# Strassen's seven products for the first MLP matrix of a transformer block, and one written list of the MLP's instructions

## Chip, cores and metric

The kernel runs on one core of a Trainium2 chip. A core has a matrix engine (TensorE, PE in the profile), a vector engine (VectorE, DVE), a scalar engine (ScalarE, ACT), GpSimd (POOL), and queues that start DMA transfers, here mostly SyncE's (SP). Each engine works through its own list of instructions in order and waits for the others by semaphores. The metric is the device time of one execution in microseconds (us).

## What is computed

One transformer block on S = 2048 tokens of width D = 640: a modulated LayerNorm, attention over a sliding window of 256 tokens with 32 heads, a residual, a second modulated LayerNorm, and an MLP with its own LayerNorm, width FF = 1536 and a GELU. All is in float32. Cut to what matters here:

```python
h = _layernorm(x) * (1 + ca) + sa
x = x + ga * _A_ref(h, A_wqkv, A_wo)          # attention, output projection
h = _layernorm(x) * (1 + cb) + sb
y = _layernorm(h)
g = gelu(y @ w1 + b1)                          # 640 -> 1536
x = x + gb * (g @ w2 + b2)                     # 1536 -> 640
```

## The kernel before

**Products in three parts.** Float32 operands are split into a high part (rounded to the matmul's type) and a low part (the rest). Each product is then three matmuls: high x high, high x low, low x high. So every operand that is made on the way costs a copy (the high part, on ScalarE or VectorE) and a subtraction (the low part, on VectorE or GpSimd).

**Tiles.** 128 tokens are a block (16 of them, `bg`), 512 tokens a chunk (4, `ch`). D is 5 tiles of 128 (KT), FF is 12 (FT). A matmul of the MLP streams 512 columns, the tokens of a chunk.

**Stages.** Attention runs first, in slots counted by `t`. Near its end the blocks of tokens go through `mid_steps(bg)` (L826): load the attention output and `x` ("load"), scale (`om`), split (`oh`, `ol`), output projection (`w00` to `w14`, ten steps of three matmuls of 320 columns), add to `x` (`add0`, `add1`), statistics (`sa0`, `sa1`), normalize (`n1`, ScalarE), modulate (`m0`, `m1`), transposes of `x` and their store (`x0`, `x1`), statistics again (`sb0`, `sb1`), normalize (`n2`), transposes of `y` and their split (`y0`, `y0l`, `y1`, `y1l`). Blocks 0 to 3 do this in the attention's last slots, block 4 partly; the others run between the matmuls of the MLP, at times from the table `MID_AT`, in units of a block: `mids` holds the steps, `fill()` hands one out after each group of three matmuls.

**MLP.** A loop over the four chunks and over the 12 tiles `f` of FF. For each: w2's tile is loaded and split, 15 matmuls make `h` (5 tiles of depth, 3 parts) in the one PSUM bank "h", ScalarE makes the GELU, VectorE splits `g`, and meanwhile `second` adds the previous `f` into the five banks `out` (15 matmuls). w1 is loaded and split once, in chunk 0, and all of its 12 tiles stay in SBUF. `close` scales the result, adds the residual and stores it. The modulation vector `gb` is made during chunk 0 (`gate`).

**What sets the order.** The attention's order comes from tables (`EXTRA`, `EARLY`, `WARM` and others). In the MLP it is the loop's order, with `mids` put in by time; on VectorE, ScalarE and GpSimd it is the order in which the program issues the instructions.

Of the kernel before, what the change touches and what calls it, by code (L numbers as in the profile page):

```python
# [35 lines left out]
MODV = 133  # L36
# [10 lines left out]
MV = [8, 9, 12, 17, 19, 21, 22, 26, 28, 29, 30]  # L47
# [16 lines left out]
SUMS_LAST = [14, 15, 18, 25, 26, 27, 29, 35, 42, 43, 50, 59, 63, 64, 74, 76, 79, 83, 86, 88, 91, 92, 95, 101, 105, 106, 110, 111, 113, 116, 117, 118, 120, 121, 122, 123, 126, 129, 131, 132, 133, 135, 136, 139]  # L64
# [5 lines left out]
WOS = [89.75, 94.0, 99.5, 109.0, 111.75, 114.25, 117.5]  # L70
W1S = [117.75, 121.75, 133.75]
# [7 lines left out]
LO0 = 4.5  # L79
PER = 4.8132  # L80
LATE = 0.8265
TAIL_AT = {'rd': -1.338, 'ri': -0.963, 'load': -0.933, 'om': -0.141, 'oh': 0.058, 'ol': 0.133, 'w00': 0.287, 'w01': 0.36, 'w02': 0.382, 'w03': 0.493, 'w04': 0.511, 'add0': 0.569, 'sa0': 0.741, 'w10': 0.711, 'w11': 0.716, 'w12': 0.726, 'w13': 0.855, 'w14': 0.865, 'add1': 0.885, 'sa1': 1.178, 'n1': 1.2, 'm0': 1.327, 'x0': 1.382, 'x1': 1.544, 'm1': 1.344, 'sb0': 1.562, 'sb1': 1.598, 'n2': 1.709, 'y0': 1.844, 'y0l': 2.007, 'y1': 2.026, 'y1l': 2.118}
MID_AT = {'rd': -1.42, 'ri': -0.884, 'load': -0.74, 'om': -0.25, 'oh': 0.081, 'ol': 0.084, 'w00': 0.336, 'w01': 0.341, 'w02': 0.367, 'w03': 0.455, 'w04': 0.495, 'add0': 0.567, 'w10': 0.643, 'sa0': 0.626, 'w11': 0.736, 'w12': 0.773, 'w13': 0.837, 'w14': 0.924, 'add1': 0.968, 'sa1': 1.042, 'n1': 1.181, 'm0': 1.223, 'm1': 1.236, 'x0': 1.314, 'sb0': 1.338, 'x1': 1.465, 'sb1': 1.467, 'n2': 1.504, 'y0': 1.802, 'y0l': 1.925, 'y1': 2.011, 'y1l': 2.093}
# [3 lines left out]
        "w12 w13,w13 w14,w14 add1,add0 sa0,sa0 sa1,add1 sa1,sa1 n1,n1 m0,m0 m1,m0 sb0,m1 sb1,sb0 sb1,sb1 n2,n2 y0,y0 y0l,"  # L87
        "y0 y1,y1 y1l,x0 x1,add1 x0,y0l y1"
# [33 lines left out]
def block_kernel(ctx: ExitStack, tc: tile.TileContext, x, wqkv, wo, w1, b1, w2, b2, c, crow, wmod, wcol, sel, outT):  # L122
# [410 lines left out]

# [25 lines left out]

# [251 lines left out]
    def r_steps(ch):  # L811

        ts, box = slice(ch * CHUNK, (ch + 1) * CHUNK), {}

        def load():
            pool, tag = (att, "rd") if ch < 2 else (base, "acc")
            box["rd"] = pool.tile([P, P if ch < 2 else D], F32, tag=tag, name=f"rd{ch}")[:, 0:P]
            nc.sync.dma_start(box["rd"], o_scr[:, DH, ts])

        def invert():  # L820
            nc.vector.reciprocal(box["rd"], box["rd"])
            nc.sync.dma_start(r_scr[:, ts], box["rd"])

        return load, invert

    def mid_steps(bg):  # L826
# [20 lines left out]
        def o_low():  # L847
            nc.gpsimd.tensor_tensor(bx["oT"][1], bx["o"], f32(bx["oT"][0]), ALU.subtract)
# [21 lines left out]
        def stats(src, nm, h):  # L870
            mid = box2["mid"]
            if h == 0:
                bx["st"] = mid.tile([P, 2, 6], F32, tag="st", bufs=2, name=f"st{nm}{bg}")
            st = bx["st"]
            nc.vector.bn_stats(st[:, h], src[:, 320 * h : 320 * h + 320])
            if h == 0:
                return
            mv = mid.tile([P, 2], F32, tag="mv", bufs=3, name=f"mv{nm}{bg}")
            rs = mid.tile([P, 1], F32, tag="rs", bufs=3, name=f"rs{nm}{bg}")
            nc.vector.bn_aggr(mv, st)  # L880
            rstd_of(rs, mv[:, 1:2])
            nr = mid.tile([P, 1], F32, tag="nr", bufs=3, name=f"nr{nm}{bg}")
            nc.gpsimd.tensor_tensor(nr, mv[:, 0:1], rs, ALU.mult)
            nc.gpsimd.tensor_scalar(nr, nr, -1.0, None, ALU.mult)
            bx[nm] = nr, rs

        def apply_(dst, src, nm):
            nr, rs = bx[nm]
            nc.scalar.activation(dst, src, AF.Identity, bias=nr, scale=rs)

        def norm1():
            bx["y"] = box2["mid"].tile([P, D], F32, tag="yb", name=f"y{bg}")
            apply_(bx["y"], bx["x"], "a")

        def mod(h):
            y, cs = bx["y"][:, 320 * h : 320 * h + 320], slice(320 * h, 320 * h + 320)
            eng = nc.vector if now[0] >= MODV and bg < len(TAIL0) or 2 * bg + h in MV else nc.gpsimd
            eng.tensor_tensor(y, y, box2["cb"][:, cs], ALU.mult)
            eng.tensor_tensor(y, y, box2["sb"][:, cs], ALU.add)

        def xtrans(k0, k1):
            def go():
                if k0 == 0:
                    bx["xT"] = box2["mid"].tile([P, KT, P], F32, tag="xT", name=f"xT{bg}")
                nc.scalar.copy(bx["xT"][:, k0:k1], turned(bx["x"], f"xt{bg}", k0, k1))
                if k1 == KT:
                    nc.sync.dma_start(x1_scr[:, :, rows].rearrange("k p t -> p k t"), bx["xT"])

            return go

        def ytrans(k0, k1):
            cs = slice(bl * P, (bl + 1) * P)

            def go():
                if ch < 2 and ch not in yT:
                    yT[ch] = [base.tile([P, KT, CHUNK], F32R, tag=f"h{i}{1 - ch}", name=f"y{i}{ch}") for i in ("hi", "lo")]
                bx["py", k0] = turned(bx["y"], f"yt{bg}", k0, k1)
                nc.scalar.copy(yT[ch % 2][0][:, k0:k1, cs], bx["py", k0])
# [574 lines left out]
```

## Time and profile before

| | |
|---|---|
| median of 3 runs | 978.35 us (977.57 to 978.8) |
| span of the profiled execution, first to last instruction | 975.4 us |
| PE busy | 945.9 us, 97% of the span |
| VectorE, ScalarE, GpSimd busy | 589.0, 445.1, 487.8 us |
| first matmul of the MLP's first product | at 576.9 us |
| matmuls of 512 columns in the MLP | 720 of the first product, 720 of the second |
| PE's mean granted clock | 0.998 |

The profile comes from one execution, and its span leaves out what lies around the first and the last instruction; its own full time is not given. A busy PE is not a PE at its peak, since matmuls overlap and their ends are modelled: how often one starts is what counts. The names in a row are those of the program's tiles, out<-in; all instructions have the line of one helper (L116), so they are told apart by tile.

### The profile page before, as it was taken

The page shows a single profiled execution, that of the slowest core. Times are in us where ns is not written, and L with a number is a line of the kernel's source. Part 1 is how long each engine was busy: PE and PEld are TensorE (multiplying, and loading weights), DVE is VectorE, ACT ScalarE, POOL GpSimd, SP SyncE. Part 2 cuts the span into 40 slices and gives each one's busy share as a digit, 9 for nine tenths or more (in the row PEclk, how much of TensorE's full clock was granted, in tenths as well). Part 3 has the DMA queues.
Part 4 walks back from the last instruction along what each step waited for, and adds up shares of the span by engine and source line. Part 5 has one row for each costly group of instructions (what it writes and reads, how often), then busy time and mean ns, then how long its engine had stood idle before and what let it go on. Part 6 is the DMA issues. An engine that isn't in the chain of part 4 may idle for free.

```text
span 975.4 us, 20091 instructions
## 1 busy us (share of the span) xinstructions
PE 945.9 (97%) x7781; PEld 751.9 (77%) x7781; DVE 589.0 (60%) x991; ACT 445.1 (46%) x781; POOL 487.8 (50%) x674
## 2 busy tenths in 40 slices
PE   8899999999999999999889999999999999999998
PEld 8777777777777777777677677888888888888886
DVE  6564977888776786767788556563544344342112
ACT  3723555666654545555545654434333243333222
POOL 3423555677864364463646844654454454332121
PEclk9999999999999999999999999999999999999999
DMA  8366778666778359854862245444413342124113
GB/s 307 97 210 197 244 228 274 188 187 170 220 226 251 114 175 283 240 157 120 226 161 76 81 142 156 127 130 138 138 57 103 115 145 85 54 58 144 54 43 119
DMA packets 98974, 152.17 MB, mean 156 GB/s; under 512 B 8864, under 2 KB 42112, under 8 KB 98880
## 3 DMA queue, kind: packets, MB, share of 16 engines
q1 hardware_dynamic: 89664, 142.50, 48.4%
q10 hardware_dynamic: 9216, 8.39, 2.7%
q8 instruction: 62, 1.02, 0.4%
q14 instruction: 32, 0.26, 0.1%
HBM read 98.51 MB, written 51.58 MB: 154 GB/s over the span
## 4 chain that ended last, share of the span: by engine, by line
PE 81%; DVE 7%; ACT 5%; DMA 2%; issue 2%; POOL 1%; SPq 1%; ACTq 0%; DVEq 0%; POOLq 0%
PE pp L116 17%; PE out L116 16%; PE h L116 16%; PE e L116 8%; PE o L116 7%; PE wo L116 6%; PE s L116 4%; ACT pt L116 3%; DVE e L116 2%; PE ppo L116 1%; SPq L116 1%; PE yt L116 1%; DVE nm L116 1%; DMA wc<-in_wcol 1%; PE xt L116 1%
## 5 line engine op out<-in xcount | busy, mean ns | idle before, releaser
L116 POOL TENSOR_SCALAR_AFFINE_SELECT pt<-pt 128x512 f32<-128x512 f32 x192 | 129.1, 672 | 128.8 <-ACT pt L116 122.0
L116 ACT ACTIVATE pt<-e 128x1024 f32<-128x1024 f32 (+1 forms) x120 | 133.7, 1114 | 64.5 <-DVE e L116 62.0
L116 DVE TENSOR_REDUCE nm<-s 128x1 f32<-128x256 f32 (+4 forms) x206 | 157.6, 796 | 4.4
L116 POOL TENSOR_TENSOR w2lo<-w2r,w2hi 128x640 fp32r<-128x640 f32 x48 | 78.5, 1635 | 163.0 <-ACT w2hi L116 163.0
L116 PE MATMUL e<-qbuf,kbuf 62*128 62x128 f32 (+2 forms) x773 | 111.8, 328 | 10.6 <-ACT pt L116 9.5
L116 DVE CAST ghi<-g 128x512 fp32r<-128x512 f32 x48 | 27.4, 571 | 155.0 <-ACT g L116 155.0
L116 PEld LDWEIGHTS e<-qbuf,kbuf 62*128 62x128 f32 x773 | 80.8, 185 | 49.8 <-ACT pt L116 25.9
L116 PE MATMUL pp<-hhi,w_hi 128*128 128x512 f32 x265 | 113.6, 429 | 0.2 <-ACT pf L116 0.2
L116 PE MATMUL s<-kbuf,qbuf 60*128 60x384 f32 (+2 forms) x728 | 105.9, 302 | 4.3 <-DVE nm L116 1.9
L116 PE MATMUL pp<-hlo,w_hi 128*128 128x512 f32 x265 | 108.3, 409 | 0.6 <-POOL hlo L116 0.6
L116 DVE COPY_PREDICATED e<-mask_t,e 128x512 f32<-128x512 uint32 x96 | 66.6, 694 | 70.0 <-PE e L116 65.8
L116 PE MATMUL pp<-hhi,w_lo 128*128 128x512 f32 x265 | 106.2, 401 | 0.0
L116 PE MATMUL o<-pt,vbuf 128*32 128x128 f32 x2688 | 99.6, 277 | 0.6 <-ACT xT L116 0.6
L116 PEld LDWEIGHTS s<-kbuf,qbuf 60*128 60x128 f32 x728 | 89.1, 186 | 14.2 <-DVE nm L116 5.9
L116 PE MATMUL out<-ghi,w2hi 128*128 128x512 f32 x240 | 95.3, 397 | 0.9 <-ACT g L116 0.9
L116 PE MATMUL out<-glo,w2hi 128*128 128x512 f32 x240 | 93.9, 391 | 0.0
L116 PE MATMUL out<-ghi,w2lo 128*128 128x512 f32 x240 | 93.8, 391 | 0.0
L116 POOL TENSOR_TENSOR w_lo<-wraw,w_hi 128x128 fp32r<-128x128 f32 x171 | 76.1, 476 | 31.4 <-ACT w_hi L116 31.4
L116 PE MATMUL h<-yhi,w1hi 128*128 128x512 f32 x220 | 87.6, 398 | 0.0
L116 PE MATMUL h<-ylo,w1hi 128*128 128x512 f32 x220 | 86.1, 392 | 0.0
L116 PE MATMUL h<-yhi,w1lo 128*128 128x512 f32 x220 | 86.0, 391 | 0.0
L116 DVE COPY_PREDICATED s<-mask_t,s 128x512 f32<-128x512 uint32 x112 | 77.1, 688 | 13.8 <-PE s L116 13.5
(179 smaller groups left out, 1838.3 us busy)
## 6 DMA issues: line engine op xcount, KB each, us to landing
w2r<-in_w SPq DMA_DIRECT2D x48, 320.0 KB
qbuf<-q_scr SPq DMA_DIRECT2D x60, 240.0 KB
wraw<-in_wqkv SPq DMA_DIRECT2D x36, 320.0 KB
kbuf<-k_scr SPq DMA_DIRECT2D x44, 240.0 KB
q_scr<-stage SPq DMA_DIRECT2D x20, 512.0 KB
k_scr<-stage SPq DMA_DIRECT2D x20, 512.0 KB
o_scr<-oT ACTq DMA_DIRECT2D x64, 128.0 KB
wm<-in_wmod SPq DMA_DIRECT2D x20, 320.0 KB
```

The source lines that it names most:

```text
L116: return self.tc.keep_in_program_order(op(*args, **kw))
```

## The change

The first product of the MLP is made for two chunks, A and B, at once. With w1 cut into two halves of FF (6 tiles each, `HF`) and the depth cut into tiles 0 and 1 on one side and 2, 3, 4 on the other, it is a 2 x 2 block product, and Strassen's scheme (in the form of Winograd) makes it of seven products, P1 to P7, instead of eight:

- P1 and P2 use w1 and chunk A as they are. P1 is copied to SBUF (`p1`), P2 is added to it (`a2`), which gives the first six tiles of A.
- P3 to P7 use sums and differences of w1's blocks (`w1_sums` on VectorE or GpSimd, five instructions; split by `ws_high`, `ws_low`) and of the chunks' blocks (`combine`: `raw`, `t1`, `t2`, `t3`, `t4` and the split of t1 and t2; `ra`, `th`, `tl` for chunk A's side). Their results are put together by `a6`, `a7`, `b5`, `a5`, `a4`, `a3` (VectorE, one operand in PSUM), and the GELU follows (`e5`, `e4`, `e3`).

For each pair of chunks there are three parts: the P1/P2 part, with chunk A's second product; the middle part with P6, P5, P7, P4, P3 for each of six `i` (54 matmuls each, 15 of them of the second product); and a last part with the second product of chunk B alone. P1, P2, P4, P6 and P7 use the bank "h", P5 and P3 the bank "t".

w1 no longer stays in SBUF: it is loaded and split again for each pair. `mid_steps` is cut into finer pieces; `n1` goes, and `m0` and `m1` become one VectorE instruction each over 640 columns, with the normalization in them; the scaling `om` and the low parts `ol` go to VectorE for some blocks.

The instructions of the MLP are one list, `PLAN`: a word is one step, a number is that many groups of three matmuls. Some entries of the attention's tables (`SUMS_LAST`, `WARM`, `WOS`, `W1S`, `TAIL_AT`, `NEXT`) shift as well.

```diff
-WARM = {(115, 0): 2, (121, 0): 2, (127, 2): 1, (130, 1): 4, (135, 0): 5, (136, 0): 10}
+WARM = {(115, 0): 1, (121, 0): 3, (127, 2): 1, (130, 1): 2, (135, 0): 4, (136, 0): 10, (114, 3): 6, (120, 3): 1, (135, 2): 1}
-NEXT = 134.05
-CROSS = 1.07
+NEXT = [133.869, 138.565]
+CROSS = [1.165, -0.035]
+PLAN = """
+w1d2 w2d1 gl3 gl4 gl0 gl2 load.6b gl1 1 w1h01 1 w2h0 m0.4 x0.4a p100 w2l0 w1l01 w1h02 w2h1 m1.4 1 w1d3 oh.5 w2d2
...
+"""
+COMB = {"raw": "p", "t1": "p", "t1h": "d", "t1l": "d", "t3": "p", "t2": "p", "t2h": "d", "t2l": "d", "t4": "p"}
+SPAN = [0, 0, 0, 0, 0, 2, 1, 1, 0, 0, 0, 0, 0, 2, 1, 1]
+OME = 'pppdpppppddddddp'
+OLE = 'pppppdpdpddddddd'
...
         def mod(h):
-            y, cs = bx["y"][:, 320 * h : 320 * h + 320], slice(320 * h, 320 * h + 320)
-            eng = nc.vector if now[0] >= MODV and bg < len(TAIL0) or 2 * bg + h in MV else nc.gpsimd
-            eng.tensor_tensor(y, y, box2["cb"][:, cs], ALU.mult)
-            eng.tensor_tensor(y, y, box2["sb"][:, cs], ALU.add)
+            mean, rs = bx["a"][0][:, 0:1], bx["a"][1]
+            if h == 0:
+                bx["y"] = box2["mid"].tile([P, D], F32, tag="yb", name=f"y{bg}")
+                nc.vector.scalar_tensor_tensor(bx["y"], bx["x"], mean, box2["cb"], ALU.subtract, ALU.mult)
+            else:
+                nc.vector.scalar_tensor_tensor(bx["y"], bx["y"], rs, box2["sb"], ALU.mult, ALU.add)
...
+                if name == "raw":
+                    for z, t in enumerate((b0, b1)):
+                        eng.tensor_tensor(t, *(f32(y[:, 2 * z : 2 * z + 2, cs]) for y in yT[1]), ALU.add)
+                elif name == "t1":
+                    eng.tensor_tensor(a0, b0, a0, ALU.subtract)
+                elif name == "t3":
+                    eng.tensor_tensor(b0, b1, b0, ALU.subtract)
+                elif name == "t2":
+                    eng.tensor_tensor(b1, b1, a0, ALU.subtract)
+                elif name == "t4":
+                    eng.tensor_tensor(a1, a1, b1, ALU.subtract)
...
+        for i in range(HF):
+            j, w = 2 * FT * p + HF + i, ("ws", p, i)
+            product(("P6", p, i), hb, (w, 0, "yB", 0), (w, 1, "yB", 1))
+            second(j - 1, [0])
+            product(("P5", p, i), pb, (w, 2, "t1", 0), (w, 3, "t1", 1), (w, 11, "yB", 4))
+            product(("P7", p, i), hb, (w, 4, "yA", 0), (w, 5, "yA", 1))
+            second(j - 1, [1, 2])
+            product(("P4", p, i), hb, (w, 9, "yA", 2), (w, 10, "yA", 3), (w, 11, "yA", 4))
+            product(("P3", p, i), pb, (w, 6, "yB", 2), (w, 7, "yB", 3), (w, 8, "yB", 4))
+            second(j - 1, [3, 4])
```

**GpSimd while block 5 and 6 are made ready, before.** `w2lo` is the low part of a tile of w2, `ob` the scaled attention output, `ot_lo` its low part, `rsa` and `nra` small values of the normalization, `y` the modulation.

```order
L116 TENSOR_TENSOR w2lo0_3_8143<-w2r3_8044,w2hi0_3_8142 128x640
L116 TENSOR_TENSOR ob6_8064<-ob6_8064,r6_8066 128x640
L116 TENSOR_TENSOR w2lo0_4_8219<-w2r4_8144,w2hi0_4_8218 128x640
L116 TENSOR_TENSOR rsa5_8234<-rsa5_8234,mhalf_68 128x1
L116 TENSOR_TENSOR nra5_8238<-mva5_8233,rsa5_8234 128x1
L116 TENSOR_SCALAR nra5_8238<-nra5_8238 128x1
L116 TENSOR_TENSOR ot6_lo_8245<-ob6_8064,ot6_hi_8244 128x640
L116 TENSOR_TENSOR y5_8258<-y5_8258,cb_b_6285 128x320
L116 TENSOR_TENSOR y5_8258<-y5_8258,sb_b_6286 128x320
```

**GpSimd at the end of the P1/P2 part, now.** `rb0` and `ra0` are the block sums of the pair (`raw`, `t1` to `t4`), `w1s00lo` and `w1s01lo` low parts of summed weights, `ylo0` chunk A's low part (`tl00`).

```order
L193 TENSOR_TENSOR w1s00lo_8507<-w1r7_8248,w1s00hi_8506 128x384
L193 TENSOR_TENSOR w1s00lo_8507<-cm00_8275,w1s00hi_8506 128x1152
L193 TENSOR_TENSOR w2lo5_8558<-w2r5_8288,w2hi5_8557 128x640
L193 TENSOR_TENSOR rb0_0_7988<-yhi1_7902,ylo1_7903 128x2x128
L193 TENSOR_TENSOR rb0_1_7989<-yhi1_7902,ylo1_7903 128x2x128
L193 TENSOR_TENSOR ra0_1_7987<-ra0_1_7987,rb0_1_7989 128x2x128
L193 TENSOR_TENSOR ra0_0_7986<-rb0_0_7988,ra0_0_7986 128x2x128
L193 TENSOR_TENSOR rb0_0_7988<-rb0_1_7989,rb0_0_7988 128x2x128
L193 TENSOR_TENSOR rb0_1_7989<-rb0_1_7989,ra0_0_7986 128x2x128
L193 TENSOR_TENSOR ra0_1_7987<-ra0_1_7987,rb0_1_7989 128x2x128
L193 TENSOR_TENSOR ylo0_7107<-rb0_0_7988,yhi0_7106 128x1024
L193 TENSOR_TENSOR w1s01lo_8678<-w1r9_8591,w1s01hi_8677 128x384
```

The modulation has left GpSimd, and the sums of blocks and the low parts of summed weights have come, in one row behind each other; the ninth of these rows is t2 of block 7, the last of the sums that P6 needs.

**TensorE between two tiles of the first product in chunk 0, before.** `h0_6` is the product for f = 6, `wo6` the output projection of block 6, `yhi0` and `ylo0` chunk 0.

```order
L116 MATMUL wo6_1_8371<-wo_hhi_6291,ot6_hi_8244 128x320
L116 MATMUL wo6_1_8371<-wo_hlo_6292,ot6_hi_8244 128x320
L116 MATMUL wo6_1_8371<-wo_hhi_6291,ot6_lo_8245 128x320
L116 MATMUL h0_6_8413<-yhi0_7103,w1hi6_7914 128x512
L116 MATMUL h0_6_8413<-ylo0_7104,w1hi6_7914 128x512
L116 MATMUL h0_6_8413<-yhi0_7103,w1lo6_7925 128x512
```

**TensorE at the first of the middle products, now.** `P6_0_0` is P6 of the first pair, `yhi1` and `ylo1` chunk 1, `w1s00` summed weights, `wo9` the output projection of block 9.

```order
L193 MATMUL wo9_0_8661<-wo_hhi_6291,ot9_hi_8413 128x320
L193 MATMUL wo9_0_8661<-wo_hlo_6292,ot9_hi_8413 128x320
L193 MATMUL wo9_0_8661<-wo_hhi_6291,ot9_lo_8414 128x320
L193 MATMUL P6_0_0_8691<-yhi1_7902,w1s00hi_8506 128x512
L193 MATMUL P6_0_0_8691<-ylo1_7903,w1s00hi_8506 128x512
L193 MATMUL P6_0_0_8691<-yhi1_7902,w1s00lo_8507 128x512
```

After six tiles of FF the first product needed chunk 0 alone; now it needs chunk 1, and so block 7 at that place.

**TensorE in the middle part, now, from P7 to P4** (fourth `i` of the first pair; both are written to the bank "h").

```order
L193 MATMUL P7_0_3_9156<-yhi0_7106,w1s03hi_9017 128x512
L193 MATMUL P7_0_3_9156<-ylo0_7107,w1s03hi_9017 128x512
L193 MATMUL P7_0_3_9156<-yhi0_7106,w1s03lo_9018 128x512
L193 MATMUL out_0_1_8053<-ghi8_9119,w2hi8_9029 128x512
L193 MATMUL out_0_1_8053<-glo8_9120,w2hi8_9029 128x512
L193 MATMUL out_0_1_8053<-ghi8_9119,w2lo8_9030 128x512
L193 MATMUL out_0_2_8079<-ghi8_9119,w2hi8_9029 128x512
L193 MATMUL out_0_2_8079<-glo8_9120,w2hi8_9029 128x512
L193 MATMUL out_0_2_8079<-ghi8_9119,w2lo8_9030 128x512
L193 MATMUL P4_0_3_9179<-yhi0_7106,w1s03hi_9017 128x512
```

Before, fifteen matmuls of the second product stood between two uses of that bank; here there are six.

More of the change, by code (lines that the diff above doesn't have):

```diff
@@ L21 @@
 FT = FF // P
+HF = FT // 2
 HALF = 1024
@@ new lines, in block_kernel, with later, mm, go @@
+    pe, aux, at, tl = [], [], {}, {}
+    y_tiles(1)
+    tl["yA"], tl["yB"] = yT[0], yT[1]
+    def later(time, go):
+        aux.append((time, len(aux), go))
+    def mm(bank, shape, w, x, first, last):
+        def go():
+            if first:
+                pool, tag = shape
+                tl[bank] = pool.tile([P, CHUNK], F32, tag=tag, name="_".join(str(b) for b in bank))
+            (whi, wlo), (xhi, xlo) = w(), x()
+            matmul(tl[bank], whi, xhi, start=first, stop=False)
+            matmul(tl[bank], whi, xlo, start=False, stop=False)
+            matmul(tl[bank], wlo, xhi, start=False, stop=last)
+        pe.append(go)
@@ new lines, in both, with product, second @@
+    def both(key, *at_):
+        return lambda: [t[(slice(None), *at_)] for t in tl[key]]
+    def product(name, shape, *parts):
+        at[name, 0] = len(pe)
+        for n, (wk, w, yk, kt) in enumerate(parts):
+            mm(name, shape, both(wk, w), both(yk, kt), n == 0, n == len(parts) - 1)
+        at[name] = len(pe)
+    jobs = []
+    def second(j, ms):
+        if j < 0:
+            return
+        ch, i = divmod(j, FT)
+        for m in ms:
+            if m == 0:
+                at["x", j] = len(pe)
+            mm(("out", ch, m), (ps_out, f"o{m}"), both(("w2", j), slice(m * P, (m + 1) * P)), both(("g", j)), i == 0, i == FT - 1)
+        if ms[-1] == KT - 1:
+            at["e", j] = len(pe)
@@ new lines, in block_kernel @@
+    hb, ob, pb = (ps_h, "h"), (ps_out, f"o{KT - 1}"), (pools["t"], "t")
+    for p in range(2):
+        at["pair", p] = len(pe)
+        for f in range(HF):
+            first = (("P1", p, f), ob if not p and f == 1 else hb, *((("w1", p, f), kt, "yA", kt) for kt in range(2)))
+            rest = (("P2", p, f), ob if not p and f == 1 else hb, *((("w1", p, f), kt, "yA", kt) for kt in range(2, KT)))
+            j = 2 * FT * p + f
+            if not p and f < 2:
+                if f == 0:
+                    firsts, rests = [first], [rest]
+                    continue
+                for each in firsts + [first] + rests + [rest]:
+                    product(*each)
+                second(0, range(KT))
+                continue
+            product(*first)
+            second(j - 1, range(2))
+            product(*rest)
+            second(j - 1, range(2, KT))
+        at["mid", p] = len(pe)
+        for i in range(HF):
[8 more added lines that the diff above has]
+            second(j - 1, [3, 4])
+        at["last", p] = len(pe)
+        for i in range(FT):
+            second(2 * FT * p + FT + i - 1, range(KT))
@@ L1451 @@
+    for _, bg, gos, nm in mids:
+        for n, go in enumerate(gos):
+            ops[f"{nm}.{bg}" + "abc"[n] * (len(gos) > 1)] = go
+    for word in PLAN.split():
+        if word in ops:
+            ops.pop(word)()
+        else:
+            for _ in range(int(word)):
+                pe.pop(0)()
+    assert not ops and not pe
 def kernel(A_x, A_wqkv, A_wo, B_x, B_w1, B_b1, B_w2, B_b2, c, w_mod):
```

466 lines of the change are left out of this document (323 added, 143 removed).

## The prediction

> **What bounds the kernel now.** I began with the page's head, then read the busy time of each engine by stretches of the span, then the chain of work that ended last.
>
> ```profile
> span 975.4 us, 20091 instructions
> PE 945.9 (97%) x7781; PEld 751.9 (77%) x7781; DVE 589.0 (60%) x991; ACT 445.1 (46%) x781; POOL 487.8 (50%) x674
> ```
>
> The stretches (us, then for each engine its busy time and instructions, granted TensorE clock, DMA share, GB/s) show that TensorE is never free in the MLP:
>
> ```profile
> 600.00:650.00 50.00, 50.00 (x263) 43.03 (x262) 32.24 (x52) 20.66 (x33) 31.96 (x32) 1.00 0.40 125
> 900.00:950.00 50.00, 50.00 (x222) 41.40 (x221) 7.85 (x14) 10.37 (x15) 12.54 (x8) 1.00 0.16 47
> ```
>
> The chain gives the price of a matmul: fifteen in a row, of either product, take 3.40 us, which is 0.2267 us each. The 389 ns that the trace shows for one is its length with the pipeline's overlap, and must not be multiplied.
>
> ```profile
> 923.65 3.40 PE out L116 x15
> 927.05 3.40 PE h L116 x15
> ```
>
> Who waits is the next view. TensorE's waits between 560 and 600 us are these two; after 600 us it has none.
>
> ```profile
> PE out L116 <- ACT g L116: 0.9, 1, 0.9
> PE wo L116 <- POOL ot_lo L116: 0.7, 1, 0.7
> ```
>
> So removed matmuls count in full, and so does every new wait.
>
> **What is removed.** The first product of two chunks has 2 x 12 x 5 x 3 = 360 matmuls of 512 columns. The seven block products have 2+3+2+3+2+3+3 = 18 steps of three for each of six pairs of column blocks, 324. Two pairs of chunks: 72 fewer (the programs' order has 720 before and 648 now; the second product keeps its 720). 72 x 3.40/15 = **16.3 us** less. The saving is a tenth and not an eighth, since five blocks of depth split into two and three.
>
> The Trainium skill, page "TensorE: Matmul & The Clock Gate", section "Back-to-back issue gap", gives about 131 ns for a sustained matmul of 512 columns; by it the saving would be 9.4 us. The chain's 227 ns differs, and the measurement decides.
>
> **What is added, and where it lies.** Adding and subtracting blocks goes to VectorE, GpSimd and ScalarE. The stage that matters is the first one of the MLP: TensorE does six P1 and P2 products and the second product for five blocks, while blocks 4 to 7 of tokens are made ready, since P6, the first of the middle products, needs all of chunk 1. Before, those blocks had 12 such steps of time, now half.
>
> TensorE's own work up to P6: 55 steps of three matmuls, 37.4 us; 44 steps of the output projection; 40 transposes; the gate. Prices of the last two kinds:
>
> ```profile
> 567.65 0.60 PE L116 MATMUL xt<-idn,xb 128*128 128x128 f32 x4
> 568.00 0.39 PE L116 MATMUL wo<-wo_hhi,ot_hi 128*128 128x320 f32 x1
> ...
> 572.25 0.31 PE L116 MATMUL wo<-wo_hhi,ot_hi 128*128 128x320 f32 x1
> ...
> 572.98 0.31 PE L116 MATMUL wo<-wo_hhi,ot_lo 128*128 128x320 f32 x1
> ```
>
> Five projection matmuls take 0.73 us, so a step of three takes 0.44 and 44 take 19.3 us; four transposes take 0.35 us, so 40 take 3.5. With about 1 us for the gate that is **61 us**.
>
> Now the other side. VectorE and GpSimd do not run freely beside each other:
>
> ```profile
> 584.45 0.82 DVE L116 TENSOR_TENSOR w1lo<-w1r,w1hi 128x640 fp32r<-128x640 f32 x1 [1.53 <-ACT w1hi L116]
> ...
> 591.87 1.55 POOL L116 TENSOR_TENSOR ot_lo<-ob,ot_hi 128x640 fp32r<-128x640 f32 x1 [0.84 <-ACT ot_hi L116]
> 592.45 1.65 DVE L116 TENSOR_TENSOR w1lo<-w1r,w1hi 128x640 fp32r<-128x640 f32 x1 [2.85 <-ACT w1hi L116]
> 593.38 2.15 POOL L116 TENSOR_TENSOR w2lo<-w2r,w2hi 128x640 fp32r<-128x640 f32 x1
> 594.02 1.86 DVE L116 TENSOR_TENSOR y<-y,cb_b 128x320 f32<-128x320 f32 x1
> ```
>
> The same VectorE subtraction takes 0.82 us alone and 1.65 when GpSimd is inside an instruction: it ends 0.68 us after GpSimd does (594.10 against 593.42). GpSimd's next then ends 1.43 us after that instead of 1.57. They take turns, and a change of hands saves 0.14 us. The spread of the durations (min/median/max) shows which VectorE work is held up: subtractions of two SBUF tensors and fast copies are, a sum with an operand in PSUM (xb<-wo) never is.
>
> ```profile
> L116 DVE TENSOR_TENSOR glo<-g,ghi x48: 691/693/1943, 582.2 to 965.7; 128x512 fp32r<-128x512 f32 x48
> L116 DVE CAST ghi<-g x48: 408/428/1296, 581.4 to 965.3; 128x512 fp32r<-128x512 f32 x48
> L116 DVE TENSOR_TENSOR w1lo<-w1r,w1hi x11: 814/825/2189, 578.6 to 667.2; 128x640 fp32r<-128x640 f32 x11
> L116 DVE TENSOR_TENSOR xb<-wo,xb x32: 467/491/492, 499.0 to 855.5; 128x320 f32<-128x320 f32 x32
> L116 DVE SCALAR_TENSOR_TENSOR acc<-wm,sil,acc x12: 872/959/1314, 107.4 to 348.4; 128x640 f32<-128x640 f32 x12
> L116 POOL TENSOR_TENSOR w2lo<-w2r,w2hi x48: 1557/1568/2185, 580.4 to 961.7; 128x640 fp32r<-128x640 f32 x48
> L116 POOL TENSOR_TENSOR stage<-pf,stage x27: 1266/1282/1292, 54.7 to 462.9; 128x512 fp32r<-128x512 f32 x27
> ```
>
> and GpSimd's short ones (count, then busy us and mean ns):
>
> ```profile
> L116 POOL TENSOR_TENSOR w_lo<-wraw,w_hi 128x128 fp32r<-128x128 f32 x171 | 76.1, 476 | 31.4 <-ACT w_hi L116 31.4
> L116 POOL TENSOR_TENSOR rsb<-rsb,mhalf 128x1 f32<-128x1 f32 x16 | 10.1, 632 | 19.4 <-DVE rsb L116 19.4
> L116 POOL TENSOR_SCALAR nrb<-nrb 128x1 f32<-128x1 f32 x16 | 4.1, 259 | 1.4
> L116 POOL TENSOR_TENSOR nrb<-mvb,rsb 128x1 f32<-128x1 f32 x16 | 3.1, 196 | 1.3
> ```
>
> GpSimd's list up to t2 of block 7 (256 columns by the line from 0.476 at 128 to 1.28 at 512: 0.75): 7 low parts of weights and 5 of om/ol at 1.57, 18.8; one glo, 1.3; six block sums of 512 columns, 7.7; eleven of 256, 8.2; the low part of the first summed weights (384 + 1152 columns), 3.7; powers and small ones, 6.2. Together 45.9 us in 47 instructions. VectorE's held kind: m0 and m1 of four blocks, 8 x 0.87; five gate sums, 4.4; four w1 and five om/ol, 7.4; two sets of weight sums, 4.0 (1.04 ns a column from 0.49 at 320 and 0.69 at 512); two sums of 1024 columns, 2.4; three ghi, 1.3; four glo, 2.8; five low parts of t1 and t2, 2.6. Together 31.9 us in 46. The two lists take turns: 77.8 us, and 64.8 if hands changed at each of the 93. TensorE has 61 us in that time, so P6 waits between 4 and 17 us; the middle is 10. Then t2's low part of block 7 stands behind tl00 on GpSimd, 1024 columns or 2.4 us, if that starts first. Behind P6 stands every later matmul, since TensorE's list is fixed; nothing makes the pause good. I take **+12** for both together (ends 0 and 18; 0 if VectorE and GpSimd run ahead of TensorE at the start).
>
> The same sum before the second pair's P6, from block 14's last powers on: GpSimd 27.9 us in 27, VectorE 11.1 in 20, so 39.0 or, with all hand-overs, 32.4; TensorE has 44 steps and the last transposes and projections, 33. I take **+3.5** (0 to 8). In the second-product stretch between them the two lists are 58.7 against TensorE's 58.3 and hand-overs make room: **+1.5** (0 to 4) for a late transpose.
>
> The middle steps have one bank ("h") for P6, P7 and P4. Between P7 and P4 stand six matmuls, 1.36 us and one more start, 0.23. What must happen there:
>
> ```profile
> 930.06 0.39 PE L116 MATMUL h<-yhi,w1lo 128*128 128x512 f32 x1
> 930.53 0.69 ACT L116 ACTIVATE g<-h,b_sb 128x512 f32<-128x512 f32 x1 [2.90 <-PE h L116]
> 931.26 0.43 DVE L116 CAST ghi<-g 128x512 fp32r<-128x512 f32 x1 [5.64 <-ACT g L116]
> ```
>
> The last matmul's result is read 0.47 us after its start; the sum u3 takes about 0.72 (PSUM operand, so not held up) and the next engine starts 0.05 later: 1.24 of 1.59 us. It fits by 0.35 if VectorE is free. I take **+1** (0 to 5) for twelve such places.
>
> Edits that I cost at nothing: the last twelve steps of a pair need w2 twice as fast, a 320 KB piece every 3.40 us. One is issued at 936.11 and has landed before 938.60:
>
> ```profile
> 936.11 13.93 SPq L116 DMA_DIRECT2D w2r<-in_w  x3
> ...
> 938.60:939.10 0.50, 0.50 (x4) 0.41 (x3) 0.50 (x1) 0.00 (x0) 0.00 (x0) 1.00 0.00 0
> ```
>
> and its halves (ACT, then 1.57 us on GpSimd) fit into one step with two buffers; if SyncE's queue, now mixed with w1 pieces and block loads, were late by one, each late piece costs its lateness, 0 to 3 us in all. Attention's shifted table entries, n1 gone from ScalarE and mods moved to VectorE touch a part where TensorE's waits are on ScalarE's exponentials (520 to 560 us: total, times, longest):
>
> ```profile
> PE e L116 <- ACT pt L116: 2.6, 4, 1.0
> ```
>
> They could go or double: 0, ends -3 and +3. The end (five sums, five stores) is the same code order.
>
> **Clock.** After a pause TensorE can lose speed:
>
> ```profile
> 10.00:20.00 10.00, 8.57 (x57) 8.13 (x56) 8.43 (x30) 4.75 (x7) 7.43 (x12) 0.83 1.04 396
> ```
>
> 0.17 of 10 us is 1.7 us after one pause. Two pauses of P6 may bring it back: **+1** (0 to 3). The Trainium skill, same page, section "What's actually happening", halves the clock after an idle window of about 3.4 us; by it each pause longer than that would add 1.7 us, an estimate, and the row agrees in size.
>
> **Sum.** -16.3 + 12 + 3.5 + 1.5 + 1 + 1 = +2.7 us on the span of 975.4: 978.1. The median of the runs, 978.35, stands 2.95 us over the span, for what lies around it; so **981.0 us**.
>
> **Rivals.** *The additions are hidden*: if turn-taking costs as little as hand-overs allow and both engines start early, only some 3 us of waits remain: 978.35 - 16.3 + 3 = 965, between 962 and 974. For it speaks that each engine's sum alone fits in 61 us (GpSimd 45.9; VectorE 31.9 and some 23 of statistics and sums from PSUM); against it the rows above, where they wait for each other. It decides if P6 starts less than 3 us late. *The single bank*: glo, when held up, lasts 1.94 instead of 0.69 us; if that stands in front of u3, P4 is late by 1.25 - 0.35 = 0.9 us, 11 us in twelve places, and the like before P2 adds some: 981 - 1 + 11 to 16, say 991. It decides if VectorE is more than 0.35 us late after P7. Against it: u3's neighbours in the order are PSUM sums. *The change removes less than it says* is excluded by the count of matmuls in the order.
>
> **Chances.** A measurement of this kernel can tell about 0.2% from no change, 2 us: faster is under 976.4, slower over 980.3. Taking turns (975 to 988): 0.60, of which slower 0.40, same 0.16, faster 0.04. Hidden: 0.26, faster 0.24, same 0.02. Single bank: 0.14, slower 0.12, same 0.02. So faster 0.28, same 0.20, slower 0.52. The ends of the unknown costs reach from 959 to 1006 together; leaving one in ten on each side I take 966 to 992, and for the likeliest case alone 975 to 988.
>
> **What would show it.** A wait of PE on P6 of the first pair, released by VectorE or GpSimd, of some 10 us, near 61 us after the first P1, and a lesser one before the second pair's P6; VectorE subtractions of twice their length there; no idle TensorE in the middle steps. PE's busy matmuls must fall by 72. I would be wrong if P6 starts on time, if waits are spread over all P4, or if the waits stand in attention.

## The result and the profile after

| | before | after |
|---|---|---|
| median | 977.96 us (4 runs, 977.5 to 978.8) | 1002.68 us (4 runs, 1001.14 to 1003.91) |
| profiled execution: own time, span | span 975.4 us | 1001.14 us, span 999.4 us |
| mean granted clock of TensorE | 0.998 | 0.992 |

The changed kernel takes 1.0252 times as long (95% interval 1.0238 to 1.0267), 24.7 us more, where the prediction was 2.7 us more and its range ended at 992.

First the page's head of the changed kernel, as for the one before.

```profile
span 999.4 us, 20268 instructions
PE 944.9 (95%) x7719; PEld 741.5 (74%) x7719; DVE 723.6 (72%) x1140; ACT 473.7 (47%) x830; POOL 534.0 (53%) x672
```

TensorE has 72 matmuls of 512 columns fewer, as counted, and ten more of the kernel's filler matmuls ahead of the MLP (`warm`, 176 instead of 166), so 62 in all. Its busy time falls by 1.0 us alone: the recorded length of a matmul is not its price, as the prediction says of the 389 ns. VectorE has 135 us more. The windows of the MLP alone (before from 577 us, after from 578; the columns are us, then each engine's busy time and instructions, clock, DMA share, GB/s) show where that went. Before:

```profile
577.00:975.40 398.40, 392.63 (x1900) 330.58 (x1900) 165.99 (x300) 134.22 (x212) 165.34 (x168) 1.00 0.35 108
```

After:

```profile
578.00:999.40 421.40, 388.28 (x1834) 316.62 (x1830) 296.33 (x446) 166.90 (x266) 222.58 (x186) 0.99 0.39 119
```

VectorE goes from 166 to 296 us in the MLP, and TensorE idles 33.1 us there instead of 5.8. What it waits for, in the same stretch (us in total, times, longest; the six largest, 26 of 28 us). `glo` is the low part of the GELU's result, `ylo` that of the MLP's input, `xb` is `x` with the output projection added, `y` ScalarE's normalization:

```profile
PE out L193 <- DVE glo L193: 7.0, 4, 2.2
PE yt L193 <- ACT y L193: 5.5, 5, 2.4
PE yt L193 <- DVE ylo L193: 5.3, 6, 1.7
PE wo L193 <- DVE xb L193: 5.1, 3, 3.3
PE xt L193 <- issue: 1.7, 4, 0.6
PE P L193 <- DVE ylo L193: 1.5, 1, 1.5
...
```

Before, this list had two waits of under 1 us. Now it is not one pause at P6 but over twenty. Of the 28 us, 21 are directly behind VectorE; the 5.5 behind ScalarE's `y` follow a block's statistics, which VectorE makes. To place them I cut the MLP at these starts of matmuls (the timeline of TensorE):

```profile
578.62 0.48 PE L193 MATMUL P<-yhi,w_hi 128*128 128x512 f32 x1
...
658.38 0.63 PE L193 MATMUL P<-yhi,w1s00hi 128*128 128x512 f32 x1
660.48 0.50 PE L193 MATMUL P<-ylo,w1s00hi 128*128 128x512 f32 x1 [1.47 <-DVE ylo L193]
...
744.59 0.39 PE L193 MATMUL P<-yhi,w1s05lo 128*128 128x512 f32 x1
...
813.43 0.39 PE L193 MATMUL P<-yhi,w1a10hi 128*128 128x512 f32 x1
...
866.51 0.39 PE L193 MATMUL P<-yhi,w1s10hi 128*128 128x512 f32 x1
...
947.38 0.39 PE L193 MATMUL P<-yhi,w1s15lo 128*128 128x512 f32 x1
```

"Own work" is the number of matmuls in a part times their spacing when nothing waits (0.227 us for 512 columns, 0.146 for a projection, 0.09 for a transpose); the rest is lost to waits and to the clock.

| part | length | own work | lost | forecast |
|---|---|---|---|---|
| P1/P2, first pair | 79.8 | 60.6 | 19.2 | 12, with the next part's first wait |
| middle, first pair | 86.2 | 83.3 | 3.0, 1.9 of it at its second matmul | 0.5 |
| second product, first pair | 68.8 | 59.6 | 9.3 | 1.5 |
| P1/P2, second pair | 53.1 | 48.3 | 4.8 | 3.5 |
| middle, second pair | 80.9 | 71.9 | 9.0 | 0.5 |
| last part, to the last matmul | 47.9 | 45.8 | 2.1 | 0 |

Together 47.4; the kernel before loses 8.2 by the same count. With 1.7 us that the MLP starts later, 47.4 - 8.2 + 1.7 - 16.3 = 24.6, against 24.0 between the spans. So the saving came in full, and 41 us went against it instead of 19. (A single profiled execution of these kernels can lie 5 us beside the median of its kernel, and the granted clock differs with it; below, totals are medians, and lengths of parts come from the profiles.)

### The profile page after: what moved, and what is told of

Its sections match the earlier page's. It is cut to its first block, busy times and chain, and to the rows that moved or that the text cites. A ratio compares the mean times of both kernels' runs of the same rounds, so it can differ in the third digit from the quotient of the medians.

```text
span 999.4 us, 20268 instructions
## 1 busy us (share of the span) xinstructions
PE 944.9 (95%) x7719; PEld 741.5 (74%) x7719; DVE 723.6 (72%) x1140; ACT 473.7 (47%) x830; POOL 534.0 (53%) x672
## 4 chain that ended last, share of the span: by engine, by line
PE 67%; DVE 18%; ACT 5%; issue 4%; DMA 3%; POOL 2%; SPq 0%; DVEq 0%; ACTq 0%; POOLq 0%
PE pp L193 16%; PE P L193 12%; PE out L193 9%; PE e L193 7%; PE o L193 7%; PE s L193 4%; PE wo L193 4%; ACT pt L193 3%; DVE e L193 3%; PE ppo L193 2%; DVE glo L193 2%; DVE nm L193 1%; DVE cm L193 1%; DMA ob<-o_scr 1%; DVE ghi L193 1%
## 5 line engine op out<-in xcount | busy, mean ns | idle before, releaser
L193 POOL TENSOR_TENSOR w2lo<-w2r,w2hi 128x640 fp32r<-128x640 f32 x46 | 81.4, 1770 | 96.3 <-ACT w2hi L193 85.7
L193 DVE COPY_PREDICATED e<-mask_t,e 128x512 f32<-128x512 uint32 x96 | 66.6, 694 | 68.8 <-PE e L193 62.5
L193 ACT COPY oT<-o 128x128 f32<-128x128 f32 x128 | 33.9, 265 | 119.1 <-PE o L193 112.1
L193 PEld LDWEIGHTS o<-pt,vbuf 128*32 128x32 f32 x2688 | 66.9, 109 | 15.0 <-issue 2.7
L193 PEld LDWEIGHTS pp<-hhi,w_hi 128*128 128x128 f32 x265 | 49.9, 188 | 20.4 <-issue 11.3
L193 ACT ACTIVATE gs<-gs,b_sb 128x512 f32<-128x512 f32 x24 | 17.4, 723 | 89.3 <-DVE gs L193 89.3
```

The costliest lines, as they stand in the source:

```text
L193: return self.tc.keep_in_program_order(op(*args, **kw))
```

## Experiments

The prediction's theory, *taking turns*: a VectorE instruction on two SBUF tensors, or a fast copy, waits while GpSimd is inside one, so what counts is both engines' lists together and when they meet. Rival: VectorE's own list is simply too long. All times are to be held against 1002.7 us of the changed kernel.

**The middle part of the second pair.** Its three waits are one picture. The timeline of the changed kernel:

```profile
893.85 2.75 POOL L193 TENSOR_TENSOR w1s13lo<-cm,w1s13hi 128x1152 fp32r<-128x1152 f32 x1
...
894.13 3.02 DVE L193 TENSOR_TENSOR glo<-gr,ghi 128x512 fp32r<-128x512 f32 x1
...
896.57 2.01 POOL L193 TENSOR_TENSOR w2lo<-w2r,w2hi 128x640 fp32r<-128x640 f32 x1
...
897.20 0.50 PE L193 MATMUL out<-glo,w2hi 128*128 128x512 f32 x1 [1.91 <-DVE glo L193]
```

GpSimd is 0.28 us inside a subtraction of 1152 columns when glo starts; glo ends 0.55 us after it, and TensorE has waited 1.91 us for glo. The Trainium skill, page "SBUF — State Buffer", section "SBUF: two separate sides", calls the port pair of these two engines an exclusive lock, held for a whole instruction; this row agrees.

mid_low_on_vector gives these subtractions to VectorE (five places of the string, the first of them still in the P1/P2 part):

```diff
-WSE = 'ppppddpppppd'
+WSE = 'ppppdddddddd'
```

> Edit: the low parts of the summed weights of the second pair's middle part (WSE, four of them: 384 + 1152 columns each) go from GpSimd to VectorE. Theory 'taking turns': glo lasted 2.77 to 3.02 us there instead of 0.69 because it waited behind GpSimd's 2.7 us subtraction; on VectorE itself that subtraction takes some 1.6 us for both pieces and comes after glo, so the three waits of TensorE for glo (2.2, 1.9, 1.9 us) and the clock lost after them (about 0.8 us each) go: 6 to 9 us less than the changed kernel, 994 to 997. Rival 'VectorE is full, whatever GpSimd does': it gets 4 x 1.6 us more in the middle part, the waits for glo stay or grow: 1002 to 1009.

Measured: 994.84 us, as taking turns had it. low_after_glo leaves every instruction on its engine and issues the split a little later, for three of the six tiles:

```diff
-... a311 sh13 1 gh31 1 gl_31 w2h32 sl13 1 e311 1 a612 ...
+... a311 1 gh31 1 gl_31 w2h32 1 e311 sh13 sl13 1 a612 ...
```

> Edit: in the list of instructions alone: in the second pair's middle part the split of the next summed weights (sh12 to sh14 and sl12 to sl14, on ScalarE and GpSimd as before) is issued some two to four groups of matmuls later, behind the GELU that follows glo. Nothing changes its engine, and no work is added or taken away. Theory 'taking turns': glo finds GpSimd free, the three waits of TensorE for it (6.0 us) and the clock lost after them go: 995 to 997. Rival 'an engine's amount of work counts': the same as the changed kernel, 1001 to 1004. If the summed weights came too late instead, P6 of the next tile would wait for w1s: 1004 or more.

Measured: 994.36 us, 0.6 under the range of taking turns and far from the rival's. The six glo of that part (ns, shortest/median/longest), in the changed kernel:

```profile
L193 DVE TENSOR_TENSOR glo<-gr,ghi x6: 683/1800/3017, 866.7 to 936.2; 128x512 fp32r<-128x512 f32 x6
```

and in low_after_glo:

```profile
L192 DVE TENSOR_TENSOR glo<-gr,ghi x6: 680/693/831, 866.6 to 927.5; 128x512 fp32r<-128x512 f32 x6
```

TensorE has no wait left there: the part takes 72.3 us instead of 80.9 and loses 0.4. The same work on the same engines in another order is worth 8.3 us, so this term is settled: it was the meeting of two instructions, not an amount of work.

**Who carries the first P1/P2 part.** VectorE is busy 70.3 of the part's 79.8 us, 88% (the 96% of the next expectation holds for 577 to 611 us). Five kernels change there which engine does what. w2low_on_vector:

```diff
-W2E = 'ppppppppppp...
+W2E = 'dddddddpppp...
```

> Edit: the low parts of the first seven tiles of w2 (W2E, in the first P1/P2 part) go from GpSimd to VectorE. Theory 'taking turns': what counts in that part is the sum of both engines' lists, and such a subtraction costs 1.57 us on GpSimd and 0.82 on VectorE, so 7 x 0.75 = 5 us less: about 997. Rival 'VectorE is full': it was busy 96% of that part, and 7 x 0.82 = 6 us more on it are 6 us more: about 1008.

Measured: 997.12 us; but in the profile (of an execution of 1002.2 us) the part itself is only 2.3 us shorter (77.5). more_on_gpsimd moves work the other way:

```diff
-W1E = 'pddddpppdddp'
-SUME = 'ddppdpdpdddd'
+W1E = 'ppppppppdddp'
+SUME = 'ppppdpdpdddd'
```

> Edit: the reverse in the same part: four low parts of w1 and two sets of weight sums (W1E, SUME) go from VectorE to GpSimd. Theory 'taking turns': +4 x 0.75 and +2 x 1.5 us in the sum of the lists, 6 us more: about 1009. Rival 'VectorE is full': it is relieved of 4 x 0.82 and 2 x 2.0 us, 7 us less: about 995.

Measured: 1009.22 us, as taking turns asked; again the part itself changed by 1.2 us alone (80.9), and the middle part took 5.4 more. VectorE got 10.7 us less to do in the part, GpSimd 8.4 more, and the part was 11 us longer than GpSimd's busy time, as it is 9.5 longer than VectorE's in the changed kernel (busy times in the order of the windows above: VectorE 59.55, GpSimd 69.89 us):

```profile
578.26:659.20 80.94, 68.78 (x349) 58.07 (x349) 59.55 (x95) 37.41 (x65) 69.89 (x64) 0.94 0.51 159
```

ghi_on_scalar (all of `GHE` on "a"):

> Edit: all copies ghi (GHE) go to ScalarE, which was busy 47% of the span. Theory 'taking turns': a copy on VectorE was held up to 2.5 us by GpSimd (0.43 alone), together some 8 us in the three parts before the last; ScalarE's never is, so 2 to 6 us less: 997 to 1001. Rival 'VectorE is full': only the copies' own 0.43 us each come off in the P1/P2 parts, 1 to 3 us less: 1000 to 1002. If ScalarE's copy, 0.3 us longer and behind its other work, makes glo late in the last parts, it is slower by 3 or more.

Measured: 1001.09 us. The first part was 2.3 us shorter and the second middle part 3.5, but the second pair's P1/P2 part 3.9 longer; the total is in the rival's range. block_sums_on_vector (all of `COMB` on "d"):

> Edit: the sums of the chunks' blocks (COMB: raw, t1 to t4) go from GpSimd to VectorE, in both pairs. Theory 'taking turns': eleven of 256 columns before the first pair's P6 cost 0.75 each on GpSimd and 0.42 on VectorE, 3.6 us less there, and as many or fewer in the second pair's: 3 to 6 less in all, 997 to 1000. Rival 'VectorE is full': eleven times 0.42 more in each part, 4 to 9 us more: 1006 to 1011.

Measured: 1006.41 us, in the rival's range too. The part got 3.7 us shorter (76.1), as taking turns asked, but the second middle part lost 6.9 us more: its largest wait for glo grew to 3.7 us. Two of these four totals fit taking turns, but the first part itself moved by less than the totals in both. seven_low_parts_left_out asked the question without giving VectorE anything. It leaves out seven low parts of w2, so its output is not the block's; ScalarE copies the tile in their place:

```diff
+        if j < 7:
+            nc.scalar.copy(lo, wt["w2", j])
+        else:
+            engines[W2E[j]].tensor_tensor(lo, wt["w2", j], f32(hi), ALU.subtract)
```

> Edit: for the first seven tiles of w2 the low part is not computed: ScalarE writes a second copy of the tile in its place, so GpSimd has seven subtractions of 1.57 us less in the first P1/P2 part, VectorE has none more, and the number of matmuls is the same. Theory 'taking turns': the sum of both lists falls by 7 x 1.57 = 11 us, and TensorE's pauses of 19 us in that part fall by about as much: 990 to 994. Rival 'VectorE is full by its own work': VectorE's list is as it was, 1001 to 1004.

Measured: 997.52 us, between the two theories, and 77.7 us for the part in the profile (of an execution of 1001.54 us): 2 less, or 3.7 with the wait of P6's second matmul, which is gone, where the sum of both lists asked for 11. So in that part the sum of the lists is not what counts. VectorE's instructions, each against the shortest of its form and tiles, are lengthened by 18 us there, as in the changed kernel: less work on GpSimd did not mean fewer meetings. VectorE's timeline in the changed kernel shows why TensorE stops: from 577.81 to 609 us it has no gap of more than 0.12 us, and it runs like this (start, us; `wm` are sums of the gate, `gr` the GELU's input and, in place, its result):

```profile
592.82 1.51 DVE L193 SCALAR_TENSOR_TENSOR wm<-wm,sil,wm 128x640 f32<-128x640 f32 x1
594.26 0.41 DVE L193 CAST ghi<-gr 128x512 fp32r<-128x512 f32 x1
594.59 2.19 DVE L193 SCALAR_TENSOR_TENSOR wm<-wm,sil,wm 128x640 f32<-128x640 f32 x1
596.71 0.54 DVE L193 TENSOR_TENSOR ylo<-yt,yhi 128x384 fp32r<-128x384 f32 x1
597.17 1.42 DVE L193 SCALAR_TENSOR_TENSOR wm<-wm,sil,wm 128x640 f32<-128x640 f32 x1
598.51 2.17 DVE L193 TENSOR_TENSOR w1a03lo<-w1r,w1a03hi 128x640 fp32r<-128x640 f32 x1
600.61 0.48 DVE L193 TENSOR_TENSOR xb<-wo,xb 128x320 f32<-128x320 f32 x1
```

The ylo here releases TensorE at 597.30 after 0.93 us, the xb at 601.24 after 1.67 us; both stood behind sums of the gate and a low part of w1, each held up. Later the chain of waits has this, four of a set of five weight sums (`cm`) in front of a ylo:

```profile
615.03 3.92 DVE cm L193 x4
618.94 0.48 DVE ylo L193
619.42 0.04 issue
619.47 0.44 PE yt L193 x2
```

**VectorE's list, by order alone.** The gate's sums need not lie there: their result is first used in the next part. gate_later (on top of low_after_glo) moves them into the middle part, with the gate's product (`gt`, `go`) and the loads and ScalarE's bias of the residual (`xr`, `xb`), which follow it:

```diff
-... gl_0 sb1.4c w04.5 gs0 1 ... e201 gs1 ... ol.6 load.7a gs2 ... y0l.4 w13.5 gs3 ... w2h2 gs4 ... w2d7 gt xr01 1 go ...
+... 1 w2d9 w02.11 gs0 ... gs1 ... gs2 ... gs3 ... a401 gs4 ... a301 gt 1 go ...
```

> Edit, in the list of instructions alone, on top of low_after_glo (994.4): the gate (five sums of 640 columns on VectorE, 0.55 to 2.2 us each in the changed kernel, then its product and the residual's bias) moves from the first P1/P2 part to the first middle part. Theory 'VectorE's list, lengthened by turns, sets the first part': it has no gap there from 578 to 611 us, the five sums are 7.4 us of it, and it later idles 2.0 us for the gate's product; with both gone the first part is 4 to 8 us shorter, and the middle part, where VectorE is busy 54 of 86 us, takes them for nothing: 987 to 991. Rival 'the sum of VectorE's and GpSimd's lists': 5 x 0.88 = 4.4 us less, 990. Rival 'each block's chain of latency': no change, 993 to 995.

Measured: 989.80 us, which fits VectorE's list and the sum of both lists alike. The part went from 80.1 to 70.7 us, 9.4 less by order alone (8.4 with the wait of P6's second matmul, now 2.5 us), where the sum of the lists asked for 4.4; no move between engines gave as much. The middle part took 5.8 of it back. The windows of that part, in low_after_glo and in gate_later:

```profile
578.31:658.41 80.10, 67.58 (x350) 55.74 (x349) 70.61 (x109) 41.76 (x70) 61.71 (x53) 0.98 0.52 165
```

```profile
578.05:648.74 70.69, 64.72 (x339) 53.46 (x339) 61.56 (x102) 36.35 (x63) 56.55 (x50) 1.00 0.52 163
```

The part is VectorE's busy time (the third) and 9 us more, in both. ScalarE and GpSimd have some 5 us less each as well, so that VectorE's share alone did it is argued, not shown. blocks_8_to_11_later also takes away what the first part does for later blocks:

> Edit, in the list alone, on top of low_after_glo (994.4): all steps of blocks 8 to 11 that stand before the first second-product stretch are issued 60 groups of matmuls later, in the first middle part. TensorE takes 14 steps of the output projection along (6.2 us), which it makes up in the middle part without waiting; VectorE loses some 6 us and GpSimd some 6 us of the first part. Theory 'VectorE's list sets the first part': the part gets 5 to 8 us shorter, the middle 6 longer: 992 to 996. Theory 'sum of both lists': the part 10 to 12 shorter, the middle 6 longer: 988 to 991. Rival 'the middle part then waits too' (its one bank, glo behind GpSimd): 997 or more.

Measured: 1002.76 us. The part was 7.8 us shorter up to P6's first matmul, but TensorE's own work in it is 6.1 us less too, and the middle part went from 86.0 to 105.1 us, 6.1 of it the moved work. The waits:

```profile
PE P L192 <- DVE u L192: 4.4, 1, 4.4
PE P L192 <- DVE ylo L192: 4.0, 1, 4.0
PE P L192 <- ACT yhi L192: 3.8, 1, 3.8
...
```

Two of them stand before P6's first two matmuls:

```profile
650.43 0.80 PE L192 MATMUL P<-yhi,w1s00hi 128*128 128x512 f32 x1 [3.82 <-ACT yhi L192]
...
655.18 0.79 PE L192 MATMUL P<-ylo,w1s00hi 128*128 128x512 f32 x1 [3.96 <-DVE ylo L192]
```

Up to the second of these, the first part is 4.9 us shorter, less than the work that TensorE lost there, though VectorE has 11 us less to do: this run speaks against VectorE's list alone and for a block's own chain, the rival that gate_later named. Here is also the wait at P6 that the prediction looked for. The third wait is for `u`, the sum that frees the one bank. VectorE is busy 60.9 of the middle part's 105.1 us, so the amount of its work does not explain these waits; the granted clock is 0.93 there, against 1.00. Another place for the moved steps was not tried. The two together and with the moves between engines:

> Edit: gate_later and blocks_8_to_11_later together. Theory 'VectorE's list': the gains add, 985 to 990, unless the middle part begins to wait.

> Edit: gate_and_blocks_later, with seven low parts of w2 and the first pair's block sums on VectorE and six copies ghi on ScalarE (as in moved_and_reordered). VectorE now has room in the first part, so the moves should give their 6 to 7 us again: 978 to 984. If it does not, GpSimd is not what sets that part any more.

Measured: 999.74 and 996.42 us; both fell short in the same place, with 106.0 and 103.1 us in the middle part.

**The second-product stretch.** last_w2low_on_vector moves GpSimd's part of the weights there (`W2E`, 11 to 23, on "d"):

> Edit: the low parts of w2's tiles 11 to 23 (W2E), which lie in the second-product stretch of the first pair, go from GpSimd to VectorE. In that stretch TensorE loses 9.3 us, most of it waiting for a block's y or ylo; VectorE is busy 63.5 of 68.8 us, of which 11.0 are lengthened instructions (glo 7.3 of it, behind w2lo of GpSimd). Theory 'taking turns': 13 x 0.75 = 10 us come off the sum of both lists, and half or more of the 9 us of waits with them: 4 to 7 us less than the changed kernel, 996 to 999. Rival 'VectorE is full, or a block's own chain of latency sets the waits': 13 x 0.82 us more on it: the same or up to 8 us more, 1002 to 1010.

Measured: 1001.86 us, and 69.1 us for the part instead of 68.8: nothing, as the rival had it. order_alone moves two sums on VectorE (`ra10`, `ra11`, 1024 columns, 1.2 us alone and 2.19 when held up) from in front of block 12's statistics to behind them, and the gate's sums a little earlier than in gate_later:

> Edit, in the list of instructions alone: gate_later (989.8) with the gate's five sums four groups earlier in the middle part, so that its product does not wait for them (1.4 us with what follows), and the second pair's two sums of chunk A (ra10, ra11, 1024 columns each on VectorE) 9 to 14 groups later, out of the way of block 12's statistics, whose transposes TensorE waited 2.4 us for. Theory 'VectorE's list sets these places': 1 to 4 us less, 986 to 989. If a block's own chain sets the waits for y: only the gate's 1 us, 989.

Measured: 987.31 us (5 runs), in the range of VectorE's list. The wait was 2.41 us in the changed kernel:

```profile
806.72 0.55 PE L193 MATMUL yt<-idn,y 128*128 128x128 f32 x3 [2.41 <-ACT y L193]
```

and is 0.31 in order_alone:

```profile
803.30 0.55 PE L192 MATMUL yt<-idn,y 128*128 128x128 f32 x3 [0.31 <-ACT y L192]
```

The stretch is 2.0 us shorter than in gate_later (66.7). So that one wait was VectorE's order; the other 7 us of that stretch stayed. The first middle part is 94.3 us in this profile (of an execution of 989.24 us) and 91.8 in gate_later's, so what the earlier sums of the gate gave is not shown.

**Moves together.** These add what the single runs gave.

> Edit: four moves at once: low parts of the second pair's summed weights, seven low parts of w2 and the block sums to VectorE, and twelve copies ghi (first P1/P2 part, second middle part) to ScalarE. Theory 'taking turns': -7.8 and -5.5 as measured alone, -3 to -6 for the block sums, -1 to -4 for the copies: 980 to 985. If VectorE becomes full by its own work, the sum falls short: 986 to 992.

> Edit: as moved_together, and w2's low parts 11 to 23 on VectorE as well. Theory 'taking turns': a further 4 to 7 us less, 974 to 980, about the kernel before. If a block's own chain sets the waits of that stretch: no further gain or a loss.

> Edit: the later issue of low_after_glo, seven low parts of w2 on VectorE, six copies ghi of the first P1/P2 part on ScalarE, and the block sums of the first pair alone on VectorE. Theory 'taking turns', with what the runs so far gave: -7 for the order, -5.5 for w2, -3.7 for the block sums before the first P6 (76.10 against 79.76 us for the part), and no loss in the second pair, since its block sums stay: 985 to 988. VectorE is then busy throughout the first part, so more is not to be had from there.

> Edit: as moved_and_reordered, with w2's low parts 11 to 23 on VectorE and block 9's transposes one group of matmuls later in the list. In the second-product stretch of the first pair the waits are for a block's y or ylo; with GpSimd free there and the transposes later, 2 to 4 us less than moved_and_reordered, 982 to 985; if a block's own chain sets them, no change.

Measured: 992.21, 991.70, 991.49 and 991.39 us. All fell short: the sums of single gains promised 974 to 988. The first came out 0.2 over what was given for a full VectorE (986 to 992), and w2's low parts 11 to 23 on VectorE added nothing to either. In moved_and_reordered the first part takes 73.1 us; GpSimd is busy 28.3 of them and VectorE 67.4: it seems that VectorE spends on the moved instructions most of what they save in held-up time. The last run puts the moves on top of order_alone:

> Edit: order_alone, with seven low parts of w2 and the first pair's block sums on VectorE and six copies ghi on ScalarE. These moves took 6.7 us off the first part when the gate's sums were still in it (79.8 to 73.1); with VectorE's list now shorter they give 2 to 6: 982 to 986, still slower than the kernel before. If they give nothing, GpSimd no longer matters in that part.

Measured: 983.68 us (6 runs), in its range and 1.0066 times the kernel before (interval 1.0051 to 1.0081). It is the best version found, 19 us better than the changed kernel and still slower than the one before. The first part in its windows:

```profile
580.64:649.70 69.06, 63.87 (x339) 53.60 (x339) 61.55 (x119) 39.08 (x67) 27.64 (x27) 1.00 0.53 167
```

GpSimd has 27.6 us there instead of 56.5 in order_alone, VectorE 61.6 in both, and the part is 69.1 against 70.7 us.

## Why the prediction was wrong, step by step

- **-16.3 us for 72 matmuls: right.** Without waits a part takes its count times the spacing: 72.3 us against 71.9 in low_after_glo's second middle part.
- **+12 before the first pair's P6: mis-sized, and for a reason that only half holds. This is the first failed step.** The part and the wait of P6's second matmul lost 21 us. The prediction took "the two lists take turns: 77.8 us" against 61 us of TensorE, and the middle between that and 64.8. The part took 79.8, so the upper sum came near, but by luck: with 11 us off GpSimd's list (seven_low_parts_left_out) the part and that wait got 3.7 us shorter. The sum took VectorE's held kind, 31.9 us, and all of GpSimd's list, and left out VectorE's "some 23 of statistics and sums from PSUM". Those two make 54.9 us; with the lengthening (counted as above), some 18 us, they make 73, and VectorE was measured at 70.3 busy. In the nineteen profiles with seven products the part is 6 to 14 us longer than the busy time of whichever of VectorE and GpSimd has more to do there: VectorE in all but more_on_gpsimd. What these 6 to 14 us are stays open; a block's own chain, loads of blocks included, is a rival that blocks_8_to_11_later speaks for. Nor did the wait stand at P6: VectorE works through ylo and xb in order with everything else, and TensorE stopped at each.
- **+3.5 for the second pair's P6: right in size** (4.8), but not in place: the waits are at transposes behind ylo. From the same sum of both lists, that is partly luck.
- **+1.5 for the second-product stretch: the same mistake**, 9.3 lost. The prediction compared 58.7 with 58.3 us and let hand-overs make room. It left out VectorE's instructions that are not held up and the order inside a block. One wait of 2.4 us is shown to be order (order_alone); the rest is open. Moving GpSimd's weights away left the stretch at 69.1 us in last_w2low_on_vector and took it from 68.7 to 66.6 in moved_with_last, which gained nothing in total.
- **+1 for the middle steps: the step failed on the operand that it didn't follow.** It followed the bank "h" (u3 within 1.59 us) and found the right answer for it: no wait of TensorE for u3 appears. But the matmul behind P6 needs glo, and ahead of glo the list puts a GpSimd subtraction of 1152 columns. The second pair lost 9.0 us there; low_after_glo shows the cause. The first pair lost 1.1 there. The rival "single bank" named glo held up, but at 1.94 us behind an instruction of 640 columns and as a delay of u3.
- **+1 for the clock: too small.** By windows of 5 us, one minus the granted clock adds up to 3.4 us from 570 us to the last matmul, against 0.2 before.
- **0 for w2's transfers, attention and the end:** no wait for w2 appears; the MLP began 1.7 us later; the last part lost 2.1.
- **The rival "hidden" (965) fell.** Its sums, 45.9 us for GpSimd and 31.9 + 23 for VectorE, fit into 61 us only without the lengthening: the two were busy 61.5 and 70.3 us in the part.
- **The sign was right**, for roughly the right reason: additions that share VectorE and GpSimd cost more than a tenth of a product saves.

## What to carry to other kernels

When a change trades matmuls for elementwise work, add up the whole list of the engine that gets it, with PSUM work and statistics, per stretch between two points that TensorE cannot pass, and lengthen the instructions on two SBUF tensors that can meet the other engine (here by 18 us in the first part). Then follow each operand of the next matmul, not only the bank: a low part issued behind a long instruction of GpSimd cost 2 us each time, and moving six words in the order took it away. Look first for work in the full stretch that is not needed there: taking out five sums and what hangs on them gave more than any exchange between the engines.

## What was not expected of the hardware

GpSimd is lengthened too: its w2lo of 640 columns, 1.57 us as a rule, took 2.01 where glo ended 0.58 us after its start (897.15 against 896.57). So the pair of a 2.75 us subtraction and a glo cost VectorE 2.3 us and GpSimd 0.4.

Shorter pauses than I counted on cost clock. After the wait of 1.91 us at 897.20 the windows of 5 us show a clock of 0.83 twice:

```profile
890.00:895.00 5.00, 5.00 (x24) 4.05 (x22) 3.81 (x7) 3.52 (x5) 2.17 (x2) 1.00 0.27 71
895.00:900.00 5.00, 3.09 (x11) 2.23 (x10) 2.75 (x2) 0.03 (x1) 3.57 (x2) 0.83 0.24 69
900.00:905.00 5.00, 5.00 (x20) 4.06 (x19) 1.98 (x4) 0.56 (x1) 0.00 (x0) 0.83 0.15 57
...
910.00:915.00 5.00, 3.09 (x14) 2.21 (x14) 3.75 (x3) 1.07 (x2) 4.62 (x2) 1.00 0.24 69
```

0.17 of 10 us is 1.7 us, almost as much as the wait, and by 904 us TensorE's starts are that far behind their spacing; a wait of the same 1.91 us at 913.24 cost 0.1. The scatter of kernels with many pauses goes with this: w2low_on_vector ran from 996.8 us, at a mean clock of 0.994, to 1002.2, at 0.988, where the windows from 570 us on add up to 8.5 us.

Left open: what sets the remaining 7 us of the second-product stretch, what the first part takes beyond the longer list, why the MLP starts 1.7 us later, and whether letting P2 add to P1 in PSUM, which would take the sums `a2` off VectorE, would help; that was not tried.
